# A planner that counts TensorE's changes between fp32 and half precision, with due times chosen anew

## The chip, the cores and the metric

The kernel runs on one core of a Trainium2 chip. TensorE (PE) multiplies matrices, VectorE (DVE) and ScalarE (ACT) work on elements, GpSimd (POOL) does almost nothing here, and SyncE (SP) issues the transfers (DMA). The metric is the device time of one execution, in microseconds; lower is better. Several runs are made, and their median counts. One more execution is recorded by the hardware profiler, and the views below are of it.

## What is computed

A layer-normalised input `xn` (2048 positions, 512 channels) goes two ways, and the results are multiplied:

```
xn = layernorm(u)
# A: a state-space convolution along the 2048 positions
K[d, l] = real(sum_n C[d,n] * exp(dt[d]*A[d,n]*l) * dt[d]*B[d,n])
s = irfft(rfft(xn, 2L) * rfft(K, 2L))[:L] + xn * Dskip
# B: token mixing by shifts, then an MLP of width 1376
h  = gelu(layernorm(xn) @ w1)
x1 = xn + shifted(h) @ w2          # the four quarters of h shifted by +1, -1, +2, -2
b  = x1 + gelu(layernorm(x1) @ w3) @ w4
out = u + s * silu(b)
```

All inputs and the output are fp32.

## The kernel before

**The stages.** `params` makes the parameters of the states. `token_mixing` does the first layer norm, the product with `w1` (tiles `xT`, `w`, `hT`), the first stage of the input's transform (`u_stage1`, tiles `X`, `ks`, output `ue`), the product with `w2` (`hs_pair`), the scales and half-precision copies of `w3` and `w4` (`prep`, tiles `w3h` and `w4h`), and the second layer norm (`ln_second`). `tables` builds the exponentials and the sines of 16 groups of 32 channels (tiles `mag`, `pt`, `kt`, `eg`; mostly VectorE and ScalarE) and sums over the states on TensorE (`sums`: 64 small fp32 matmuls in each of 32 units, into banks `pc`), which gives `K`; it goes to memory by `kev`. `kstage1` does the first stage of `K`'s transform (`ksl`, output `k1e`). `products` does the second stage of both transforms (units named `kin` and `uin`), multiplies them (`kh`, `pr`) and starts the way back (unit `pr`, output `z1e`). `inverse` ends it (`zin`) and multiplies into `X`; `finish` adds the input and stores.

The channels come in two halves, `hf` 0 and 1: `tables(0)`, `kstage1(0)`, `products(0)`, then the same for 1. The MLP has 8 groups of 256 positions, and each has six steps `jp`: 24 matmuls with `w3h`, a gelu on ScalarE (`g`), a split into two halves-precision parts (`ghl`, ScalarE and VectorE), and 12 matmuls with `w4h` into banks `pa`. Before a group, `mlp_input` normalises and transposes it (`x1n`, `x1T`).

**The two kinds of matmul.** The products with `w3` and `w4` take half-precision operands (f16, three matmuls for each product). Everything else on TensorE is fp32, the transposes too. The units have several shapes on the array: 128*128 (MLP, transposes, `w1`, `w2`), 128*64 (`kin`, `uin`), 64*128 (`pr`), 128*32 (`kt`, `pt`), 32*64 (`ks`), 64*32 (`zin`); the first number is rows, the second columns.

**The planner.** The program above does not issue instructions. It calls `Plan.add`, which notes each unit with the engines that may do it, its cost on each, and what it depends on. Units made under `plan.together` are one piece. `due(t)` sets the due time of the units that follow: `t` from constants such as `M0 + MC*g` for the MLP, `T0 + TC*cc` for the tables, `PA`, `PB` for the products, plus an entry of `SHIFT`, one for each call of `due` (353 numbers).

`Plan.order` then plays the program through with the costs. Whichever engine can start something first takes, of the units that are ready, the one with the lowest score: its due time, plus `SWITCH` where ScalarE would have to load another table of functions, plus `PREFER`, `AVOID` and their like where a unit may go to ScalarE or VectorE. The order in which each engine took its units is the order in which `issue` writes them, so it is the order on each engine's queue. A transfer is taken to land `LAND` after it ran; a table load costs ScalarE `TABLE_LOAD` in the play. Nothing of it exists on the chip but the order and the choice of engine. All instructions come from one line of `issue`, line 310, so views by line name L310 for all, and the tiles tell them apart.

Of the kernel before, what the change touches and what calls it, by code (L numbers as in the profile page):

```python
# [11 lines left out]
F16 = mybir.dt.float16  # L12
# [71 lines left out]
class Op:  # L84
# [9 lines left out]
LATENCY = {"PE": 0.23, "ACT": 0.16, "DVE": 0.13, "SP": 0.0}  # L94
SAME = {"PE": 0.0, "ACT": 0.13, "DVE": 0.1, "SP": 0.0}
TABLE_LOAD = 1.41
DMA_RATE = 300e3
LAND, PAD = 2.45, 0.16
BASE, FINE, END = 16512, 19840, 229368

KGC, QUAD = 3.25, 0.95
WARM = 40

SHIFT = (
    -2357, -12777, -7728, -8471, -1890, -5820, 626, 2299, 7826, 2606, 3103, -2484, -1642, 1374, 635, 1552,
    -5430, 4370, -2565, 2626, -1860, 4424, 2714, -4679, -3803, -2285, -3146, -4248, -5241, 213, 2051, 3978,
    9221, 3207, 1433, -2296, -2539, -178, 2374, 2140, 9495, 265, 2415, -4317, 2024, -5695, -4424, -1536, 1044,
    -3874, -412, 1369, -3390, -64, 1033, 83, -9702, 2535, -4187, 5182, -2767, -1991, -4017, 4504, -1834, 1373,
    -7030, -1888, 1509, -961, -638, -116, -8830, -3284, -147, 833, 3202, -866, 6815, 1881, -776, -1517, 8158,
    -2771, 3388, 7167, 2300, 9228, -1206, 5040, 884, 683, 384, 6727, -5917, 5434, 3924, 949, -40, 143, 1079,  # L110
    -6875, 971, 1037, -3725, -7917, 838, -5291, -3043, -2915, -1908, 3046, -1796, 231, -7429, -6152, -1811,
    -1498, -1748, -918, 3362, -1195, 68, -5613, -1298, -4707, -5318, 3932, -9853, 445, 2154, -4838, 45, -1328,
    1607, 5499, 892, -1606, 5826, -1702, 7543, -2199, -4457, 17060, 1309, 1934, 2210, 2592, -2979, -373, -4584,
    -3271, -1323, 5435, -4525, 7358, 6315, -28, 1908, 1745, 4555, -2473, -3546, 3446, -71, 3791, 3269, 3699,
    -4728, 1638, -208, 25, -3832, -1734, -7872, -6249, 1060, 1013, 154, 1376, 711, 1802, -4989, 787, 4474,
    -3057, -6935, 5895, -975, -3716, -68, 425, -1428, -1701, -608, 7719, -860, -1822, 1535, -3182, -2129, -2825,
    8377, 4060, -1121, -638, -3207, -9351, -1721, 6415, 3544, -2559, -84, -2122, 2999, 522, -1386, 8061, 10306,
    11912, 1524, -3127, -5785, -1486, -5228, -3327, 535, -2675, 2538, 770, -868, -964, -8884, 1422, -375, -549,
    413, 674, 777, 1357, 1723, -707, 1664, 2958, 2189, 2194, -4655, 4203, 1477, -692, 7608, 1024, 2389, -6548,
    3086, 1289, 4001, -5674, -2103, -2325, 191, 2535, 7638, 5247, 3899, -3574, -7476, 10, -12299, 2768, -6779,  # L120
    -7700, 8670, -577, -2655, -5094, -2963, -6991, -1665, 4621, -1517, 976, 2193, 955, 1168, -2284, -7221, 1774,
    2110, 2001, 886, 2377, -6284, -3310, -1104, -4085, -5416, -8519, -1464, 4322, -4518, -2765, 5960, -916,
    -5164, -4685, 2304, -8462, 5438, -879, 2434, -4976, -7337, -8426, 5719, -1100, -913, -157, 3264, -3332,
    -7127, 3616, 9378, -2152, 10830, -7314, -2047, -1665, 2199, -4364, 5296, 1040, -1366, -2191, 4626, -3019,
    -2281, -367, 1901, 236, 1460, -997, 2115, 2661, -1551, -3533, -5930, 1634, 1890, 6703, 8932, 2028, -4182,
)
Q0, QC = -778.0, 0.05
SWITCH = 2279.26
PREFERP, AVOIDP = 2674.41, 272.51
PREFER, AVOID = 3332.92, 790.65  # L130
PV, T0, TC = 257.0, 396.7, 309.52
LX, LC, LP, LW, LV = -4000.0, 0.11, -3964.6, -2693.7, -3696.7
M0, MC, WC = 807.9, 710.86, 0.25
H0, HC, SC = -3530.1, 638.4, 0.22
KA, PA, PAC, FA = -1045.1, -3015.7, 0.25, 592.1
KB, PB, PBC, FB = -157.1, -136.4, 0.08, 323.0
FC = 0.29


def mlp_due(g, jp):  # L140
# [3 lines left out]
class Plan:  # L144
# [50 lines left out]

    def add(self, alts, writes, reads, table=0, nbytes=0):
        op = self.group or self.new(table, nbytes)
        op.psum = "PSUM" in str(reads[0].space) if reads else False
        for e, (cost, call) in alts.items():
            old = op.alts.setdefault(e, [0.0, []])  # L200
            old[0] += cost
            old[1].append(call)


        def after(other, name):
            if other[0] is not op:
                op.deps.add(other[0].idx)
                if other[1] != name:
                    op.alias.add(other[0].idx)

        for ap in reads:
            me = (op, ap.tensor.name)
            for c in self.cover(ap):
                if isinstance(c, str):
                    op.deps.update(self.cells[c])
                    continue
                st = self.cells.setdefault(c, [None, {}])
                if st[0] is not None:
                    after(st[0], me[1])
                if c[1] == "bank":  # L220
                    for r in st[1].values():
                        after(r, me[1])
                    st[0], st[1] = me, {}
                else:
                    st[1][op.idx] = me
        for ap in writes:
            me = (op, ap.tensor.name)
            for c in self.cover(ap):
                if isinstance(c, str):
                    self.cells.setdefault(c, []).append(op.idx)  # L230
                    continue
                st = self.cells.setdefault(c, [None, {}])
                if st[0] is not None:
                    after(st[0], me[1])
                for r in st[1].values():
                    after(r, me[1])
                st[0], st[1] = me, {}
# [12 lines left out]
    def order(self):  # L250
        ops = self.ops
        for op in ops:
            op.succ, op.n, op.ready, op.eng = [], len(op.deps), 0.0, None
        for op in ops:
            for d in op.deps:
                ops[d].succ.append(op)
        pools = {e: [] for e in self.engines}
        free = dict.fromkeys(self.engines, 0.0)

        def release(op):  # L260
            for e in op.alts:
                pools[e].append(op)

        for op in ops:
            if op.n == 0:
                release(op)
        table, dma, out = 0, 0.0, []
        while len(out) < len(ops):
            t, e = min(
                (max(free[e], min(o.ready for o in pool)), e) for e, pool in pools.items() if pool  # L270
            )
            pick, score = None, None
            for o in pools[e]:
                if o.ready <= t + 0.02:
                    v = o.vt
                    if e == "ACT" and o.table and o.table != table:
                        v += SWITCH
                    if len(o.alts) > 1:
                        on = (PREFERP, AVOIDP) if o.psum else (PREFER, AVOID)
                        v += on[e != "DVE"]  # L280
                    if pick is None or (v, o.idx) < score:
                        pick, score = o, (v, o.idx)
            for k in pick.alts:
                pools[k].remove(pick)
            pick.eng = e
            pick.cost, pick.calls = pick.alts[e]
            cost = pick.cost
            if e == "ACT" and pick.table and pick.table != table:
                table = pick.table
                cost += TABLE_LOAD  # L290
            pick.start = t
            free[e] = t + cost
            if e == "SP":
                dma = max(dma, free[e] + 0.9) + pick.nbytes / DMA_RATE
                done = dma + LAND
            else:
                done = free[e]
            out.append(pick)
            for s in pick.succ:
                s.n -= 1  # L300
                s.ready = max(s.ready, done + (SAME[e] if list(s.alts) == [e] else LATENCY[e] + PAD))
                if s.n == 0:
                    release(s)
        self.span = max(max(free.values()), dma)
        return out
# [21 lines left out]
def pe_cost(name, args):  # L327
    f = 1 if args[2].dtype == F16 else 4
    return 0.11 if name == "transpose" else columns(args[2]) * f / 2400.0 + 0.0025 * (1 + f // 4)
# [25 lines left out]
class Engine:  # L355
# [3 lines left out]
    def __getattr__(self, name):  # L359
        def call(*args, **kw):  # L360
# [6 lines left out]
            table, nbytes = 0, 0  # L367
            if self.eng == "PE":
                cost = pe_cost(name, args)
            elif self.eng == "ACT":  # L370
                cost = act_cost(args, kw)
                if name == "activation":
# [47 lines left out]
def kernel(  # L420
# [405 lines left out]
    def products(hf):  # L826
# [3 lines left out]
        for un in range(NG // (2 * nb)):  # L830
# [28 lines left out]
            for b in range(nb):  # L859
# [12 lines left out]
                V.tensor_add(z[1], z[1], t[1][:, 1])  # L872
                due()
                pz = [t[:, :DH] for t in bank[3]]
                with plan.together(cost=0.9):
                    for ri in range(2):
                        for a in range(2):
                            h = slice(64 * a, 64 * a + 64)
# [370 lines left out]
```

## Time and profile before

| | us |
|---|---|
| median of 3 runs | 673.19 |
| lowest and highest run | 671.51, 675.04 |
| the profiled execution | 671.43 |
| its span, first to last instruction | 669.7 |

The mean granted TensorE clock is 0.965 of full speed. Matmuls are pipelined, so a row of the timeline overlaps the next: the time that a unit takes of TensorE is read from the start of one row to the start of the next. Rows of a timeline have the start, the time, the engine, the line, the operation, output<-inputs, the array's rows*columns, the moving operand with its type, and the count; idle time before a row stands in brackets with what ended it.

### The profile page before, as it was taken

The page shows a single profiled execution, that of the slowest core. Times are in us where ns is not written, and L with a number is a line of the kernel's source. Part 1 is how long each engine was busy: PE and PEld are TensorE (multiplying, and loading weights), DVE is VectorE, ACT ScalarE, POOL GpSimd, SP SyncE. Part 2 cuts the span into 40 slices and gives each one's busy share as a digit, 9 for nine tenths or more (in the row PEclk, how much of TensorE's full clock was granted, in tenths as well). Part 3 has the DMA queues.
Part 4 walks back from the last instruction along what each step waited for, and adds up shares of the span by engine and source line. Part 5 has one row for each costly group of instructions (what it writes and reads, how often), then busy time and mean ns, then how long its engine had stood idle before and what let it go on. Part 6 is the DMA issues. An engine that isn't in the chain of part 4 may idle for free.

```text
span 669.7 us, 13855 instructions
## 1 busy us (share of the span) xinstructions
PE 629.2 (94%) x5526; PEld 416.4 (62%) x5526; DVE 540.2 (81%) x798; ACT 479.8 (72%) x1050; POOL 0.7 (0%) x6
## 2 busy tenths in 40 slices
PE   7699989999995998998999999999999999999984
PEld 7567758466464785665687576676675756556531
DVE  5898999999999999988999999997434155454557
ACT  3989899969849999987999999994245363223420
POOL 0000000000000000000000000000000000000000
PEclk9899979999997999998999999999999999999995
DMA  8945342421022120385343314328599468844997
GB/s 258 244 132 188 107 162 93 144 98 55 32 80 79 32 61 21 80 221 173 78 137 100 97 60 125 103 75 211 168 249 276 135 148 215 205 155 142 236 315 219
DMA packets 98063, 95.60 MB, mean 143 GB/s; under 512 B 48272, under 2 KB 77968, under 8 KB 97104
## 3 DMA queue, kind: packets, MB, share of 16 engines
q1 hardware_dynamic: 98000, 94.73, 50.2%
q8 instruction: 43, 0.70, 0.4%
q14 instruction: 20, 0.16, 0.1%
HBM read 61.16 MB, written 33.55 MB: 141 GB/s over the span
## 4 chain that ended last, share of the span: by engine, by line
PE 54%; DVE 32%; DMA 6%; ACT 4%; issue 3%; SPq 1%; DVEq 0%; ACTq 0%
PE pb L310 19%; PE pa L310 12%; PE pc L310 12%; PE pd L310 11%; DVE pt L310 10%; DVE X L310 4%; DVE kt L310 4%; DMA X<-in_A_u_dram 2%; DVE pr L310 2%; DVE ghl L310 2%; DVE stats L310 2%; DVE eg L310 2%; DMA zin<-scr_Zda 1%; SPq L310 1%; DVE pab L310 1%
## 5 line engine op out<-in xcount | busy, mean ns | idle before, releaser
L310 PE MATMUL pb<-x1T,w3h 128*128 128x256 f16 (+1 forms) x1056 | 126.0, 275 | 1.1 <-DVE w3h L310 1.1
L310 PE MATMUL pa<-w4h,ghl 128*128 128x512 f16 (+1 forms) x528 | 124.5, 383 | 1.1 <-DVE w4h L310 0.8
L310 PEld LDWEIGHTS <-w3h 128*128 128x128 f16 (+1 forms) x1056 | 102.8, 101 | 30.2 <-issue 15.4
L310 ACT ACT_TABLE_LOAD x85 | 109.1, 1283 | 2.5 <-PEq L1237 0.7
L310 PEld LDWEIGHTS <-ghl 128*128 128x128 f16 (+1 forms) x528 | 49.2, 98 | 67.5 <-issue 16.2
L310 ACT ACTIVATE mag<-par 128x64 f32<-128x64 f32 x512 | 84.0, 272 | 6.3 <-DVE pt L310 6.1
L310 PE MATMUL pc<-kt 128*32 128x64 f32 x1024 | 84.6, 415 | 0.6 <-DVE kt L310 0.6
L310 PE MATMUL pc<-pt 128*32 128x64 f32 x1024 | 78.4, 387 | 0.0
L310 PE MATMUL pb<-xT,w 128*128 128x256 f32 x256 | 61.1, 396 | 1.4 <-ACT hT L310 1.4
L310 DVE SCALAR_TENSOR_TENSOR ghl<-g,wsc,ghl 128x512 f16<-128x512 f32 (+1 forms) x48 | 35.3, 750 | 31.0 <-ACT ghl L310 30.7
L310 PEld LDWEIGHTS pb<-xT,w 128*128 128x128 f32 x256 | 50.0, 199 | 15.8 <-issue 6.8
L310 PEld LDWEIGHTS pc<-pt 128*32 128x32 f32 x1024 | 56.8, 194 | 0.1
L310 PEld LDWEIGHTS pc<-kt 128*32 128x32 f32 x1024 | 48.8, 175 | 9.6 <-issue 6.2
L310 ACT ACTIVATE g<-pb,wsc 128x512 f32<-128x512 f32 (+1 forms) x48 | 32.8, 692 | 26.8 <-PE pb L310 26.5
L310 ACT ACTIVATE ghl<-g,wsc 128x512 f16<-128x512 f32 (+1 forms) x32 | 22.6, 714 | 27.0 <-PE pa L310 26.9
L310 DVE TENSOR_TENSOR kt<-mag,kt 128x1024 f32<-128x1024 f32 x32 | 41.6, 1300 | 0.0
L310 DVE SCALAR_TENSOR_TENSOR pt<-kt,pt 128x2080 f32<-128x2080 f32 x16 | 37.7, 2359 | 0.1
L310 ACT COPY z1e<-pd 128x256 f32<-128x256 f32 x36 | 12.7, 389 | 34.0 <-PE pd L310 34.0
L310 DVE TENSOR_TENSOR pr<-pc,kh 128x512 f32<-128x512 f32 x32 | 21.0, 686 | 19.4 <-PE pc L310 16.7
L310 PE MATMUL pd<-pr,cst 64*128 64x256 f32 x256 | 36.3, 402 | 0.0
L310 ACT ACTIVATE kt<-kt,halfpi 128x2080 f32<-128x2080 f32 x16 | 33.0, 2063 | 0.0
L310 DVE COPY z1e<-pd 128x256 f32<-128x256 f32 x28 | 11.6, 441 | 25.9 <-PE pd L310 25.9
(159 smaller groups left out, 990.7 us busy)
## 6 DMA issues: line engine op xcount, KB each, us to landing
wst<-in_B_w_dram SPq DMA_DIRECT2D x20, 512.0 KB, 3.7
scr_Ud<-ue SPq DMA_DIRECT2D x16, 512.0 KB, 3.1
scr_Kfa<-k1e SPq DMA_DIRECT2D x16, 256.0 KB, 3.6
uin<-scr_Ud SPq DMA_DIRECT2D x32, 128.0 KB, 3.1
cst<-c_gp SPq DMA_DIRECT2D x16, 256.0 KB, 2.8
kin<-scr_Kfa SPq DMA_DIRECT2D x32, 128.0 KB, 2.7
scr_Zda<-z1e SPq DMA_DIRECT2D x16, 256.0 KB, 2.3
xr<-in_A_u_dram SPq DMA_DIRECT2D x16, 256.0 KB, 6.3
```

Of the source, the lines that this page charges most:

```text
L310: ins = [getattr(self.engines[op.eng], name)(*args, **kw).ins for name, args, kw in op.calls]
```

## The change

Three parts. First, the planner keeps a kind for TensorE as it keeps a table for ScalarE: 1 for units with half-precision operands, 2 for fp32. In the play, a unit of the other kind costs `TURN` = 0.1 us more, and its score is raised by `KIND`. A unit made under `together` takes the kind of its members. Second, two costs of the play: `LAND` from 2.45 to 2.75, and the `pr` unit of `products` from 0.9 to 1.0. Third, all constants of the due times and all 353 numbers of `SHIFT` have other values, and so have the weights `SWITCH`, `PREFER` and `AVOID`.

```diff
+TURN = 0.1
-LAND, PAD = 2.45, 0.16
+LAND, PAD = 2.75, 0.16
 SHIFT = (
-    -2357, -12777, -7728, -8471, -1890, -5820, 626, 2299, 7826, 2606, 3103, -2484, -1642, 1374, 635, 1552,
+    -15363, -41919, 3148, -7770, -4886, -7327, 5312, 10411, 10508, 20269, 11828, -21285, -10539, -11177, -1968,
...
-SWITCH = 2279.26
-PREFERP, AVOIDP = 2674.41, 272.51
-PREFER, AVOID = 3332.92, 790.65
-PV, T0, TC = 257.0, 396.7, 309.52
-M0, MC, WC = 807.9, 710.86, 0.25
-H0, HC, SC = -3530.1, 638.4, 0.22
-KA, PA, PAC, FA = -1045.1, -3015.7, 0.25, 592.1
-KB, PB, PBC, FB = -157.1, -136.4, 0.08, 323.0
+SWITCH = 12026.4
+KIND = 1975.3
+PREFERP, AVOIDP = 8567.89, -14706.0
+PREFER, AVOID = 10606.8, 10381.4
+PV, T0, TC = 2239.0, 2383.7, 1852.46
+M0, MC, WC = 12644.9, 2568.54, 0.07
+H0, HC, SC = -4082.3, 1063.72, 0.11
+KA, PA, PAC, FA = -6598.1, -29218.2, 0.14, 13134.1
+KB, PB, PBC, FB = 9962.3, -12822.4, 0.32, 7956.4
...
     def add(self, alts, writes, reads, table=0, nbytes=0):
         op = self.group or self.new(table, nbytes)
+        op.table = op.table or table
...
-        table, dma, out = 0, 0.0, []
+        table, dma, out = {"ACT": 0, "PE": 2}, 0.0, []
+        change = {"ACT": (SWITCH, TABLE_LOAD), "PE": (KIND, TURN)}
...
-                    if e == "ACT" and o.table and o.table != table:
-                        v += SWITCH
+                    if e in table and o.table and o.table != table[e]:
+                        v += change[e][0]
...
-            if e == "ACT" and pick.table and pick.table != table:
-                table = pick.table
-                cost += TABLE_LOAD
+            if e in table and pick.table and pick.table != table[e]:
+                table[e] = pick.table
+                cost += change[e][1]
...
             if self.eng == "PE":
                 cost = pe_cost(name, args)
+                table = 1 if args[2].dtype == F16 else 2
...
-                with plan.together(cost=0.9):
+                with plan.together(cost=1.0):
```

## What I expect, before seeing the result

> **What bounds the kernel now.** I read the page's busy totals, clock line and chain first, then the busy time by stage, and then TensorE's timeline, since the change names TensorE.
>
> ```profile
> span 669.7 us, 13855 instructions
> PE 629.2 (94%) x5526; PEld 416.4 (62%) x5526; DVE 540.2 (81%) x798; ACT 479.8 (72%) x1050; POOL 0.7 (0%) x6
> PEclk9899979999997999998999999999999999999995
> PE 54%; DVE 32%; DMA 6%; ACT 4%; issue 3%; SPq 1%; DVEq 0%; ACTq 0%
> ```
>
> TensorE is busy 94% of the span and carries 54% of the chain that ended last, VectorE 32%. The clock line dips in several slices. The stretches say where each engine sets the pace.
>
> ```profile
> 90.00:211.00 121.00, 115.34 (x1018) 75.10 (x1006) 120.70 (x163) 102.69 (x298) 0.00 (x0) 0.98 0.27 88
> 211.00:226.00 15.00, 11.71 (x78) 9.70 (x79) 15.00 (x16) 12.88 (x15) 0.00 (x0) 0.68 0.15 49
> 226.00:400.00 174.00, 168.59 (x1749) 116.01 (x1748) 169.02 (x195) 162.24 (x347) 0.00 (x0) 0.99 0.36 101
> 400.00:640.00 240.00, 239.43 (x2064) 150.18 (x2063) 140.70 (x231) 124.50 (x230) 0.00 (x0) 1.00 0.66 177
> 640.00:670.00 30.00, 17.71 (x194) 5.83 (x192) 19.34 (x32) 3.57 (x4) 0.00 (x0) 0.73 0.86 254
> ```
>
> The columns are PE, PEld, DVE, ACT, POOL busy us, granted clock, DMA share and GB/s. From 90 to 226 VectorE is full (135.7 of 136 us). From 226 to 400 TensorE, VectorE and ScalarE are all within 7% of full. From 400 to 640 TensorE is full at full clock (239.43 of 240), and the other two have 100 us to spare. There only less TensorE time can shorten the kernel. The last 30 us are a tail of TensorE remnants, VectorE additions and output transfers.
>
> **What the change removes and adds.** No operation is added to or taken from the list: the 5526 matmuls, their shapes and transfers stay. What moves is the order in which each queue takes units, whether ScalarE or VectorE does a unit that both can do, and with it how many of ScalarE's table loads there are. So the sum has two terms: fewer changes on TensorE, and holes filled or opened by a new order.
>
> **Term 1, the changes on TensorE.** What one costs:
>
> ```profile
> 501.42 1.46 PE L310 MATMUL pa<-w4h,ghl 128*128 128x512 f16 x6
> 502.72 1.47 PE L310 MATMUL pb<-x1T,w3h 128*128 128x256 f16 x12
> ...
> 550.30 1.47 PE L310 MATMUL pa<-w4h,ghl 128*128 128x512 f16 x6
> 551.70 1.08 PE L310 MATMUL pc<-uin,cst 128*64 128x256 f32 x8
> 552.72 1.14 PE L310 MATMUL pd<-pr,cst 64*128 64x256 f32 x8
> 553.78 1.08 PE L310 MATMUL pc<-kin,cst 128*64 128x256 f32 x8
> 554.80 1.47 PE L310 MATMUL pa<-w4h,ghl 128*128 128x512 f16 x6
> ```
>
> A start-to-start distance is what a unit takes of TensorE. Six half-precision matmuls take 1.30 us before more halves (501.42 to 502.72) and 1.40 before fp32 (550.30 to 551.70): entering fp32 costs 0.10. A lone spectrum unit takes 1.02 (551.70 to 552.72), and a pr unit between two others 1.06.
>
> ```profile
> 406.74 1.08 PE L310 MATMUL pd<-kin,cst 128*64 128x256 f32 x8
> 407.65 1.03 PE L310 MATMUL pd<-uin,cst 128*64 128x256 f32 x8
> 408.62 2.79 PE L310 MATMUL pb<-x1T,w3h 128*128 128x256 f16 x24
> ...
> 514.00 5.34 PE L310 MATMUL pa<-w4h,ghl 128*128 128x512 f16 x24
> 519.18 0.60 PE L310 MATMUL pb<-ident,x1n 128*128 128x128 f32 x4
> 519.62 1.47 PE L310 MATMUL pb<-x1T,w3h 128*96 128x256 f16 x12
> ```
>
> Two spectrum units in a row take 1.88 (406.74 to 408.62), so two that are joined save 2 x 1.02 - 1.88 = 0.16 and one entry of 0.10: 0.26 together. But the transposes of x1n are fp32 and cost nothing on either side: 24 pa before them take 5.18, or 0.216 each, as in 1.30 / 6, and four transposes take 0.44. They have the 128*128 shape of most of the halves (the last MLP tile has 96 columns or rows). And pr followed by kin, both fp32, costs 1.06, no less than a unit that halves follow. So what is paid for is the change of the array's shape, not of the number format. Joining two fp32 units of different shapes saves the one entry, 0.10, and no more.
>
> The Trainium skill says this too: "TensorEngine Tiling (Array Packing)", Key Properties, has a change of tiling mode, not of the tile alone, drain TensorE. By that rule the planner's count of formats misses fp32 units that follow each other in different shapes, and charges the transposes for nothing; the rows above agree on both.
>
> How many there are: I read TensorE's timeline from the first unit of halves to the last.
>
> ```profile
> 217.16 10.99 PE L310 MATMUL pb<-x1T,w3h 128*128 128x256 f16 x84
> ...
> 625.29 0.66 PE L310 MATMUL pd<-zin,is 64*32 64x256 f32 x16
> 625.75 0.64 PE L310 MATMUL pc<-zin,is 64*32 64x256 f32 x16
> 626.32 1.48 PE L310 MATMUL pb<-x1T,w3h 128*128 128x256 f16 x12
> 627.73 0.66 PE L310 MATMUL pd<-zin,is 64*32 64x256 f32 x16
> 628.33 1.47 PE L310 MATMUL pa<-w4h,ghl 96*128 96x512 f16 x6
> ...
> 646.65 2.77 PE L310 MATMUL pa<-w4h,ghl 128*128 128x512 f16 x12
> 649.34 0.66 PE L310 MATMUL pd<-zin,is 64*32 64x256 f32 x16
> ```
>
> Between these ends there are 74 runs of halves, so 148 changes; 135 of them change the shape as well. Of the fp32 runs, 9 are a stage-1 unit of the kernel's transform (ksl) alone, 8 an inverse unit (zin) alone, 8 a pr alone, 3 a kin and 3 a uin alone. Two zin joined take 1.03 (625.29 to 626.32), a single one 0.60 (627.73 to 628.33): joining saves 0.17 and an entry, 0.27. If the 9 ksl become 4 runs, the 8 zin 3, the six lone spectra 3, and the 8 pr join spectra of another shape: 5 x 0.27 + 5 x 0.27 + 3 x 0.26 + 8 x 0.10 = 4.3 us. That is the upper end; below, it is nothing, or a loss as in the slower rival. The pr units cannot all be joined: in the first half pr, kin and uin of the next block share TensorE's banks d and wait for the copies out of them, and halves fill that wait. I take 2.5 us, about 60%, since some of the ksl runs lie before 400, where VectorE and ScalarE are nearly as full and TensorE's gain is not the end's. The weight on a change, KIND = 1975, is only a ninth of the spread of the new SHIFT (18,265 standard deviation, from the diff), so it decides among units that are nearly equal. That speaks for a small number of joins, unless the due times do the joining.
>
> **Term 2, the order.** The largest hole of TensorE behind the first 90 us:
>
> ```profile
> 206.09 0.61 PE L310 MATMUL pc<-pt 128*32 128x64 f32 x8
> 212.90 1.97 PE L310 MATMUL pd<-ident,x1n 128*128 128x128 f32 x8 [6.20 <-ACT x1n L310]
> 216.26 1.11 PE L310 MATMUL pd<-ident,x1n 128*128 128x128 f32 x4 [1.39 <-ACT x1n L310]
> ```
>
> TensorE has run out of table sums, and the MLP cannot begin until VectorE has finished the second layer norm behind table work. It idles 6.20 + 1.39 = 7.6 us, and the clock falls: 0.68 granted over the 15 us of the row above, 4.8 us of full-speed work lost. Together 12.4 us. Filling it needs the layer norm's VectorE work earlier, or table work that feeds TensorE kept for it; the new constants move both (M0 to T0, H0, HC). A hole filled there is worth its full price only if VectorE, full up to 226, isn't later for it. Bounds: 12.4 gained to the same lost, if it doubles. I take a third, 4 us: VectorE's 169 of 174 us in the next stretch takes most of a gain back. The tail I leave as it is: its additions hang on each other whatever the order. The first 90 us I leave too, as inputs land there.
>
> Table loads move with the order as well:
>
> ```profile
> L310 ACT ACT_TABLE_LOAD x85 | 109.1, 1283 | 2.5 <-PEq L1237 0.7 <-PE pb L310 0.4
> ```
>
> At 1.28 us each, the 11.8 us that ScalarE has to spare between 226 and 400 cover some 9 more; ten fewer there would free 13 us of ScalarE, with VectorE still full beside it. I put nothing on them; their effect either way is inside the bounds of the holes.
>
> The planner's other prices (2.75 instead of 2.45 us for a transfer to land, 1.0 instead of 0.9 for pr) move nearer to rows: pr takes 1.06. They cost no instruction; their effect is in term 2.
>
> **Sum.** 671.43 (the profiled execution; its span is 669.7, so 1.7 lie around it) - 2.5 - 4 = 664.9. The median of the three runs is 673.19, 1.8 above the profiled one, so I expect 666.7 for a median.
>
> **The rivals.**
> First, that it doesn't do what it says: kinds run longer, but shapes change as often, fp32 to fp32, at the same 0.10, and the holes only move. For it: the transposes, and the shape changes between fp32 units that the planner still counts as free. Against it: joins of equal shape do save 0.26. Then 0 to 1 us: 672.5.
>
> Second, the hole is closed entirely: 12.4 from it and 4.3 from joins are 16.7; 673.19 - 16.7 = 656.5. For it: the MLP's start depends on layer-norm work of few instructions, which a due time can bring forward. Against it: VectorE is full on both sides. "TensorE: Matmul & The Clock Gate" of the Trainium skill, Part 1, gives about 3.4 us of idling before the clock halves. The trace agrees that 6.2 was enough; a gap cut below that would keep the clock, which is in the 12.4 already.
>
> Third, slower: the halves are spent too early. They are the filler while the second half's spectra are being written and read back:
>
> ```profile
> 523.37 2.79 PE L310 MATMUL pb<-x1T,w3h 128*128 128x256 f16 x24
> 526.09 1.08 PE L310 MATMUL pc<-uin,cst 128*64 128x256 f32 x8
> 527.11 8.04 PE L310 MATMUL pb<-x1T,w3h 128*128 128x256 f16 x72
> 534.98 6.64 PE L310 MATMUL pa<-w4h,ghl 128*128 128x512 f16 x30
> 541.54 1.08 PE L310 MATMUL pc<-kin,cst 128*64 128x256 f32 x8
> ```
>
> For 14.4 us (527.11 to 541.54) TensorE runs nothing but halves, with one uin unit done and the first kin unit still to come. It decides when less than 14.4 us of halves is ready at that point, for example because runs were lengthened before it. If half of them are missing, TensorE idles 7.2 us, and the clock takes a loss like the 4.8 above: +12; less 2.5 for joins, 682.7. Against it: from 523.4 to the end the timeline holds 288 pb and 168 pa, at 7.87 / 72 = 0.109 and 0.217 us, 68 us in all, nearly five times what is needed. But halves are ready only as fast as ScalarE and VectorE evacuate the ones before, and a new order may have left fewer.
>
> **How the numbers follow.** About half a per cent, 3.4 us, is what a measurement of this kernel can tell from no change. The forecast (666.7, and its neighbours to 669.8) gets 0.42, the hole closed 0.20, no fewer shape changes 0.20, the filler spent early 0.18. So faster 0.62, same 0.20, slower 0.18. The range takes in the forecast and both rivals up to the edge of the third: below, 656.5 less the 1.7 between the lowest run (671.51) and the median; above, 673.19 and 3.8, a third of the 12 us that the third rival would cost. That is 654.8 to 677.0, and leaves 0.18 out.
>
> **What would show it.** The changes of format between the first half and the last in TensorE's timeline: about 148 less 30 to 50 if term 1 is right, with ksl and zin units in rows of two or more; the shape changes among fp32 units beside them. Unit prices must stay (0.109, 0.217, 1.02, 1.06). Term 2: the wait of pd for x1n, now 7.6 us, at some 5, and the clock there above 0.68. The third rival would show as a wait of TensorE for kin or uin behind the last ksl. I am wrong if TensorE's idle time grows elsewhere by what the hole loses, or if the tail behind the last half, now 20 us (649.3 to 669.7), is not the same.

## The result and the profile after

The changed kernel takes 669.71 us (median of 19 runs, 666.94 to 671.56) beside 672.16 us of the kernel before on the same chips (19 runs, 670.92 to 675.04). The ratio is 0.9947, with a 95% interval of 0.9935 to 0.9960: faster by half a per cent, some 3.6 us. The forecast was 666.7 in a range of 654.8 to 677.0, so the direction was right and the gain about half of what I expected. Its profiled execution took 666.94 us, the lowest of the 19, so the two profiles lie 4.5 us apart where the medians lie 2.5 apart and the ratio says 3.6.

The head of the page of the changed kernel, with its span, busy totals, clock in 40 slices and chain by engine:

```profile
span 665.2 us, 13827 instructions
PE 627.9 (94%) x5526; PEld 416.4 (63%) x5526; DVE 537.5 (81%) x794; ACT 467.3 (70%) x1043; POOL 0.7 (0%) x6
PEclk9889979999998999999999999999999999999995
PE 44%; DVE 43%; DMA 4%; issue 4%; ACT 4%; SPq 1%; DVEq 0%
```

TensorE has the same 5526 matmuls and 1.3 us less busy time. The totals of VectorE and ScalarE fell by 2.7 and 12.5 us; 11 table loads fewer (74, at 1.28 us each) are 14 us less, more than the whole fall of ScalarE. The share of the chain moved from TensorE to VectorE.

The busy time by stretch, in the columns of before:

```profile
211.00:226.00 15.00, 12.81 (x94) 10.86 (x95) 14.96 (x16) 14.58 (x17) 0.00 (x0) 0.78 0.14 45
226.00:400.00 174.00, 167.53 (x1759) 116.56 (x1758) 172.42 (x201) 154.18 (x349) 0.00 (x0) 1.00 0.39 105
400.00:640.00 240.00, 239.67 (x2080) 149.71 (x2077) 135.28 (x224) 122.17 (x223) 0.00 (x0) 1.00 0.67 187
640.00:670.00 30.00, 13.93 (x154) 4.75 (x152) 16.42 (x27) 1.57 (x2) 0.00 (x0) 0.73 0.53 148
```

The picture is that of before: TensorE full from 400 to 640, VectorE nearly full ahead of that. The hole is still there, a little shorter, with the clock at 0.78 instead of 0.68. (The clock is of one execution only: in the second profiles used below, the same stretch has 0.72 in the changed kernel and 0.71 in the one before.) Its rows in TensorE's timeline, with the idle time in brackets:

```profile
211.47 1.97 PE L318 MATMUL pd<-ident,x1n 128*128 128x128 f32 x8 [5.45 <-DVE x1n L318]
214.85 1.09 PE L318 MATMUL pd<-ident,x1n 128*128 128x128 f32 x4 [1.41 <-ACT x1n L318]
```

6.86 us of idling instead of 7.6; 6.24 in the second profile, where the kernel before has 7.6 again.

And the number that the change is about: read from TensorE's timeline, 140 changes of format instead of 148, and 129 of them with a change of shape instead of 135. The shape changes between two fp32 units rose from 82 to 85. So the changes of shape fell from 217 to 214 over the whole kernel. (The expectations below count them in the plan, unit by unit, and have 211 for these 214.)

**Where the difference lies.** Three marks of the timelines cut each profile in three: the start of the first matmul of the MLP, the start of the last one (w4h), and the end of the span. A second profile of each kernel (the runs before_again and again below) shows how far the pieces hold.

| us | before | before_again | changed | again |
|---|---|---|---|---|
| start to the first MLP matmul | 217.2 | 217.0 | 215.7 | 216.4 |
| from there to the last MLP matmul | 431.9 | 431.8 | 430.5 | 431.2 |
| from there to the end of the span | 20.6 | 20.6 | 18.9 | 18.7 |
| span | 669.7 | 669.4 | 665.2 | 666.3 |

Between the means of the pairs: 1.05 us ahead of the MLP, 0.97 in the long middle, 1.80 in the tail. The tail's part can be read from VectorE's additions of the input (X<-X,xr), eight of them, one for each pair of output rows, and each followed by its output transfer. First the changed kernel's timeline, then that of the kernel before, each from the first addition near the last MLP matmul to the last one:

```profile
637.86 1.22 DVE L318 TENSOR_TENSOR X<-X,xr 128x1024 f32<-128x1024 f32 x1
645.66 1.23 DVE L318 TENSOR_TENSOR X<-X,xr 128x1024 f32<-128x1024 f32 x1
...
657.32 1.23 DVE L318 TENSOR_TENSOR X<-X,xr 128x1024 f32<-128x1024 f32 x1
659.30 1.23 DVE L318 TENSOR_TENSOR X<-X,xr 128x1024 f32<-128x1024 f32 x1
```

```profile
647.59 1.23 DVE L310 TENSOR_TENSOR X<-X,xr 128x1024 f32<-128x1024 f32 x1
651.43 1.21 DVE L310 TENSOR_TENSOR X<-X,xr 128x1024 f32<-128x1024 f32 x1
...
661.81 1.23 DVE L310 TENSOR_TENSOR X<-X,xr 128x1024 f32<-128x1024 f32 x1
663.80 1.23 DVE L310 TENSOR_TENSOR X<-X,xr 128x1024 f32<-128x1024 f32 x1
```

At the end a pair leaves every 1.98 us (657.32 to 659.30). The changed order has one pair out at 637.86, ahead of the last MLP matmuls; the kernel before has none out until 647.59. One pair fewer in the row of 1.98 us steps is the size of what the tail gained, 1.8. TensorE's timeline has the same: six zin units behind the last half in the changed kernel (646.55 to 657.01), seven in the kernel before (649.34 to 661.50).

### The profile page after: what moved, and what is told of

It reads as the page before. It is cut to its first block, busy times and chain, and to the rows that moved or that the text cites. A ratio compares the mean times of both kernels' runs of the same rounds, so it can differ in the third digit from the quotient of the medians.

```text
span 665.2 us, 13827 instructions
## 1 busy us (share of the span) xinstructions
PE 627.9 (94%) x5526; PEld 416.4 (63%) x5526; DVE 537.5 (81%) x794; ACT 467.3 (70%) x1043; POOL 0.7 (0%) x6
## 4 chain that ended last, share of the span: by engine, by line
PE 44%; DVE 43%; DMA 4%; issue 4%; ACT 4%; SPq 1%; DVEq 0%
DVE pt L318 14%; PE pb L318 13%; PE pa L318 11%; PE pc L318 11%; PE pd L318 8%; DVE kt L318 7%; DVE X L318 4%; DVE pr L318 3%; DMA X<-in_A_u_dram 2%; DVE eg L318 2%; DVE pab L318 2%; DVE stats L318 2%; DVE ghl L318 2%; ACT L318 1%; SPq L318 1%
## 5 line engine op out<-in xcount | busy, mean ns | idle before, releaser
L318 PE MATMUL pa<-w4h,ghl 128*128 128x512 f16 (+1 forms) x528 | 121.9, 380 | 0.0
L318 PE MATMUL pb<-xT,w 128*128 128x256 f32 x256 | 63.1, 404 | 3.5 <-DMA w<-in_B_w_dram 1.9
L318 PEld LDWEIGHTS pc<-kt 128*32 128x32 f32 x1024 | 48.2, 176 | 12.4 <-issue 8.8
L318 ACT ACTIVATE ghl<-g,wsc 128x512 f16<-128x512 f32 (+1 forms) x40 | 27.4, 689 | 27.7 <-PE pa L318 27.5
L318 ACT COPY z1e<-pd 128x256 f32<-128x256 f32 x42 | 14.5, 385 | 37.3 <-PE pd L318 32.1
L318 DVE SCALAR_TENSOR_TENSOR pt<-kt,pt 128x2080 f32<-128x2080 f32 x16 | 40.4, 2523 | 0.1
L318 DVE TENSOR_TENSOR pr<-pd,kh 128x512 f32<-128x512 f32 x32 | 23.6, 749 | 13.8 <-ACT kh L318 12.1
```

Source lines behind the costliest of these rows:

```text
L318: ins = [getattr(self.engines[op.eng], name)(*args, **kw).ins for name, args, kw in op.calls]
```

## The experiments

### What a change of format costs, and what a change of shape

Matmuls without a use are put behind the last output:

```diff
...
+    with plan.together():
...
+        for a, b in ((H, F128), (H, F64), (H, H64), (F128, F64)):
+            for n in (1, 8):
+                for k in range(8 // n):
+                    for f in (a, b):
+                        for i in range(n):
+                            f()
```

> The changed kernel, with matmuls behind the last output: 12 halves of 128x256 on the full array (H), 4 fp32 on the full array (F128), 8 fp32 on 128x64 tiles (F64), 12 halves on 128x64 tiles (H64). Four pairs, each eight times in turn and then eight of the one and eight of the other: 14 changes fewer. If a change of shape is what costs, taking turns is longer by about 14 x 0.1 = 1.4 us for H and F64, H and H64, F128 and F64, and by nothing for H and F128. If a change of number format is what costs (the planner's view), it is longer by 1.4 us for H and F128 and for H and F64, and by nothing for H and H64 and for F128 and F64.

Three of the pairs in TensorE's timeline, first in turn, then eight and eight. H and F128 differ in format alone:

```profile
694.43 1.89 PE L318 MATMUL pc<-X,ident 128*128 128x256 f32 x8
696.15 1.47 PE L318 MATMUL pa<-w3h 128*128 128x256 f16 x12
697.47 1.89 PE L318 MATMUL pc<-X,ident 128*128 128x256 f32 x8
699.20 10.64 PE L318 MATMUL pa<-w3h 128*128 128x256 f16 x96
709.67 13.98 PE L318 MATMUL pc<-X,ident 128*128 128x256 f32 x64
...
723.49 1.47 PE L318 MATMUL pa<-w3h 128*128 128x256 f16 x12
```

H and H64 differ in shape alone, and F128 and F64 too:

```profile
787.53 1.49 PE L318 MATMUL pa<-w3h 128*128 128x256 f16 x12
788.94 0.85 PE L318 MATMUL pb<-w3h 128*64 128x256 f16 x12
789.72 1.48 PE L318 MATMUL pa<-w3h 128*128 128x256 f16 x12
791.14 0.84 PE L318 MATMUL pb<-w3h 128*64 128x256 f16 x12
791.91 10.65 PE L318 MATMUL pa<-w3h 128*128 128x256 f16 x96
802.50 5.43 PE L318 MATMUL pb<-w3h 128*64 128x256 f16 x96
807.86 1.99 PE L318 MATMUL pc<-X,ident 128*128 128x256 f32 x8
809.78 1.95 PE L318 MATMUL pd<-X,ident 128*64 128x256 f32 x16
811.66 1.99 PE L318 MATMUL pc<-X,ident 128*128 128x256 f32 x8
...
838.27 14.08 PE L318 MATMUL pc<-X,ident 128*128 128x256 f32 x64
852.28 14.03 PE L318 MATMUL pd<-X,ident 128*64 128x256 f32 x128
```

Format alone: a pair in turn takes 3.04 us (694.43 to 697.47), and 10.47 / 8 + 13.82 / 8 = 3.04 in blocks. It costs nothing. Shape alone, in halves: 2.19 in turn (787.53 to 789.72), 10.59 / 8 + 5.36 / 8 = 1.99 in blocks; 0.20 for a pair, 0.10 for a change. Shape alone, in fp32: 3.80 in turn (807.86 to 811.66), 14.01 / 8 + 14.03 / 8 = 3.50 in blocks (no row follows the last block, so its 14.03 is the row's own time; the same block of the pair H and F64 takes 13.97 from start to start, which gives 3.50 too); 0.15 for a change. Both together (H and F64, 3.29 in turn against 3.07) are no dearer than shape. So the planner's TURN has the right size, on the wrong thing. The rule of the Trainium skill that the prediction named ("TensorEngine Tiling (Array Packing)", Key Properties) is that a change of tiling mode drains TensorE. The trace agrees in all three pairs, as time is lost where the shape changes and nowhere else.

### Joining units of one shape

A pass behind the planner takes a TensorE unit earlier, where the plan has it ready and that joins two of one shape. Only TensorE's queue changes.

```diff
+            if shape(b) != a:
+                for j in range(i + 1, min(i + 1 + reach, len(pe))):
+                    c = pe[j]
+                    if shape(c) != a or c.ready > b.start + slack:
+                        continue
+                    if any(pos[d] >= pos[b.idx] for d in c.deps):
+                        continue
+                    if changes(pe[:i] + [c] + pe[i:j] + pe[j + 1 :]) < changes(pe):
+                        out.remove(c)
+                        out.insert(out.index(b), c)
+                        break
...
-        for op in self.order():
+        for op in self.joined(self.order(), 4, 0.5):
```

> The changed kernel, and behind the planner a pass that takes a TensorE unit up to four places earlier where that joins two units of one shape and the plan has it ready; the orders of the other queues stay. In TensorE's order 211 changes of shape become 166 and 140 changes of format 102. If changes cost TensorE time that the end waits for, 45 x 0.1 = 4.5 us less at most than the changed kernel, 2 to 4.5 with some of them before 400 us: a ratio to the kernel before of 0.988 to 0.992. Rival: a unit that is taken earlier keeps one waiting that ScalarE or VectorE needs, and the gain is given back: 0.994 or more.

Measured: 1.0132 of the kernel before (1.0093 to 1.0170), 13 us slower than the changed kernel. The rival's bound (0.994 or more) holds, but far more than the gain was given back. The busy time of its stretch from 400 to 640, its longest waits of TensorE behind 400 (the second and third lie mostly in the tail, and the changed kernel has such waits there too), and one place in the timeline:

```profile
400.00:640.00 240.00, 229.50 (x1980) 148.05 (x1979) 131.79 (x214) 117.92 (x233) 0.00 (x0) 1.00 0.61 168
```

```profile
PE pd L349 <- ACT z1e L349: 3.7, 6, 0.8
PE pd L349 <- DVE X L349: 3.1, 3, 1.6
PE pc L349 <- DVE X L349: 2.7, 2, 2.1
```

```profile
563.85 1.13 PE L349 MATMUL pd<-pr,cst 64*128 64x256 f32 x8
565.73 1.13 PE L349 MATMUL pd<-pr,cst 64*128 64x256 f32 x8 [0.75 <-ACT z1e L349]
566.79 1.08 PE L349 MATMUL pc<-kin,cst 128*64 128x256 f32 x8
567.71 1.03 PE L349 MATMUL pc<-uin,cst 128*64 128x256 f32 x8
568.57 1.08 PE L349 MATMUL pc<-kin,cst 128*64 128x256 f32 x8
570.20 1.08 PE L349 MATMUL pc<-uin,cst 128*64 128x256 f32 x8 [0.56 <-DVE pr L349]
```

TensorE is busy for 229.50 instead of 239.67 us. Two pr units in a row wait 0.75 us for ScalarE to copy the first out of the bank; a fourth spectrum unit in a row waits 0.56 for VectorE to read the one whose bank it takes. A join that saves 0.10 to 0.26 costs 0.5 to 0.8 where the unit taken out from between had covered such a copy. Between the first MLP matmul and the last, TensorE idles 20.2 us instead of 7.0; 11.5 us of that are 19 waits for VectorE or ScalarE to empty a bank (z1e, X, pr, kh, k1e), and the changed kernel has none of these there.

With moves past one unit only, and no slack:

> As the run with joined units, but a unit is moved past one other unit only, and only if the plan has it ready at that unit's start: 194 changes of shape instead of 211, 128 of format instead of 140. If what cost 13 us there is cover that was lost, and moves of this kind lose none: 17 x 0.1 = 1.7 us less than the changed kernel, 0.992. If they lose cover as well: 0.996 to 1.005.

Measured: 0.9978 (0.9956 to 1.0001), 0.3% above the changed kernel. These moves lose cover as well; the expected gain of 1.7 us isn't there. Six waits for the emptying of a bank, 3.7 us together, stand against the 17 x 0.1 = 1.7 us; the difference of 2.0 is the size of what the run is longer by.

### Far more weight on a change

```diff
-KIND = 1975.3
+KIND = 40000.0
```

> The changed kernel with KIND at 40000, twenty times as much: 86 changes of format and 166 of shape in the plan. If fewer changes are worth 0.1 us each: 45 x 0.1 = 4.5 us below the changed kernel, 0.987. If the halves between fp32 units are cover, as the run with joined units says: above 1.03, with TensorE idle behind 400 us.

720.60 us in one run, 1.07 of before. The stretch behind 640, and the longest waits of TensorE in the whole span:

```profile
640.00:720.00 80.00, 46.55 (x484) 21.51 (x480) 42.02 (x83) 10.91 (x26) 0.00 (x0) 0.77 0.89 256
```

```profile
PE pd L318 <- DMA zin<-scr_Zda: 7.0, 1, 7.0
PE pb L318 <- DVE x1T L318: 6.5, 4, 3.6
```

The MLP is done 84.8 us before the end, not 18.9: the halves came early, in long runs, and what is left is a chain of fp32 units with nothing to cover its copies and transfers. TensorE is busy for 46.55 us of the 78.8 behind 640. The wait of 7.0 us lies there, with others of 4.9 and 2.9 us for zin's transfers; those for x1T lie ahead of the last MLP matmul. This is my slower rival in kind, the filler spent early, though the transfers waited for are zin's, and not kin's or uin's as I had said. Of the weights tried in the changed kernel it shows at this one alone, twenty times the change's.

### Each part of the change without the others

The counting off, in the changed kernel:

```diff
-TURN = 0.1
+TURN = 0.0
...
-KIND = 1975.3
+KIND = 0.0
```

> The changed kernel with KIND and TURN at 0: its due times and its other costs, no counting of changes. The plan then has 142 changes of format and 212 of shape (140 and 211 with the counting). If the new due times and not the counting carry the gain, about the changed kernel's time: 0.993 to 0.997 of the kernel before. If the counting carries it, 1.000. As the due times were chosen for a plan with the counting, the other order may also be worse by chance, above 1.000.

Measured: 1.0022 (1.0003 to 1.0041). The orders in the trace are those of the changed kernel up to some 248 us, and so is the time: 215.5 us to the first MLP matmul, as there, but 436.5 from it to the last one (430.5).

The counting alone, in the kernel before (the lines of the change, with KIND at 374):

> The kernel before with the counting alone: TURN 0.1 and KIND 374, which has the same ratio to SWITCH as in the change; due times and costs as before. The plan has 160 changes of format and 222 of shape (148 and 216 before), as one other choice early moves all that follow. If the counting as such is a gain: 0.995 or less. If a due time is good only with the order it was chosen in: 1.005 to 1.03.

Measured: 1.0111 (1.0073 to 1.0150).

The two costs of the play as before, in the changed kernel:

```diff
-LAND, PAD = 2.75, 0.16
+LAND, PAD = 2.45, 0.16
...
-                with plan.together(cost=1.0):
+                with plan.together(cost=0.9):
```

> The changed kernel with the two costs of the play as before: LAND 2.45, pr 0.9. The counting and the new due times stay. The plan has 138 changes of format and 210 of shape. If the gain is of the due times and the counting: 0.993 to 0.998. If the due times are good only in the one plan that they were chosen for, as the two other partial kernels suggest: 1.005 to 1.03.

Measured: 1.0408 (1.0354 to 1.0462), worse than expected: 231.7 us to the first MLP matmul and 451.7 from it to the last.

The counting alone doesn't give the gain, and without the counting, or without the two costs, it is gone; the new due times without both weren't run. The reason that I see, argued and not shown: 353 due times fit one run of the play; another weight or cost makes one unit go first that went second, and all that follow are drawn in another order, for which the numbers were not chosen. These runs say that the parts belong together. They don't say what a part would be worth with due times of its own.

### The hole ahead of the MLP

Matmuls of the identity, which nothing reads, fill the hole in the changed kernel; the other orders stay.

```diff
         ln_second(slice(0, S))
+        vt, plan.vt = plan.vt, 1e8
+        with plan.together(cost=0.0):
+            T.matmul(bank[0][1][:, :S], ident, mv[:, :, 0], start=True, stop=True)
+            for k in range(18):
+                T.matmul(bank[0][1][:, :P], ident, ident, start=True, stop=True)
+        plan.vt = vt
```

> The changed kernel with 18 more matmuls of the identity (3.9 us at full clock) in TensorE's hole ahead of the first x1n transposes, started by the last mean and variance; nothing reads them. If the half clock behind the hole (6.8 us in the changed kernel's profile, 6.1 of them over work) is part of what sets the end, the clock stays full there and the time falls by up to 3 us: ratio to before about 0.990. If VectorE sets the pace until 400 us, nothing changes: 0.9947. If the extra matmuls hold up the transposes, it is slower than the changed kernel.

Measured: 0.9946 (0.9925 to 0.9967), the changed kernel's own. First its timeline behind the hole, then the changed kernel's:

```profile
207.84 4.26 PE L318 MATMUL pa<-ident 128*128 128x128 f32 x36
...
216.01 5.40 PE L318 MATMUL pb<-x1T,w3h 128*128 128x256 f16 x48
222.55 3.65 PE L318 MATMUL pb<-x1T,w3h 128*128 128x256 f16 x32 [1.13 <-ACT g L318]
```

```profile
215.73 6.33 PE L318 MATMUL pb<-x1T,w3h 128*128 128x256 f16 x48
222.37 5.40 PE L318 MATMUL pb<-x1T,w3h 128*128 128x256 f16 x48 [0.30 <-ACT g L318]
```

The clock stayed up at the hole: the first 48 matmuls take 5.40 instead of 6.33 us. Then TensorE waits 1.13 instead of 0.30 us for the first gelu, and both go on at the same place, 222.4 and 222.6. A wait took the place of the one removed. "TensorE: Matmul & The Clock Gate" of the Trainium skill, Part 1, asks for no idle gaps above some 3.4 us. At the hole the trace agrees: with gaps of 0.70 and 2.27 us left, the clock stayed, and that brought no time. But the limit isn't a safe one: in the same profile a stretch of 3.4 us at half clock (from 251.6) follows a gap of 1.93 us, and in the two profiles of the kernel before one (from 309.3 and 308.4) follows gaps of 1.82 and 2.01 us. The measurement decides.

The other way, 66 instead of 18:

> As the run with 18 matmuls in the hole, but with 66 (14.4 us at full clock): the first transposes and the MLP behind them start about 10 us later, with the clock full. If TensorE's time there is the end's, about 10 us less 3 for the clock: 7 us slower than the changed kernel, 1.005. If VectorE sets the pace there, at most 2 us slower: 0.995 to 0.998.

Measured: 1.0086 (1.0055 to 1.0118). The first MLP matmul is at 225.3, 9.6 later than in the changed kernel's profile, and the span is 675.2, 10.0 longer. So a delay of the MLP's start reaches the end in full, and VectorE being full there hides none of it: its own queue holds MLP units in a fixed order, and waits with them (9.1 us in one piece for x1T, where it waits for nothing between 205 and 240 us in the changed kernel). Time added to the hole has its full price. That time taken out of it would be gained in full isn't shown. The hole's clock had no price in the changed kernel, because of the gelu behind it.

### The two kernels once more

> The changed kernel once more, unchanged. Time as on record, 0.9947 of the kernel before (0.9935 to 0.996). Its profile shows how much of the difference between the two profiles (4.5 us) is of one execution: if the stretches at half clock fall otherwise in each execution, the new profile has another number of them than 7 windows of 3.4 us ahead of the tail, and another time with it; if they belong to the order, the same ones.

Measured: 0.9935 (0.9902 to 0.9967). Ahead of the tail the record of the granted clock in the trace has 27.3 us at half speed; the first profile of the same kernel had 23.9. The stretches come in steps of 3.4 us and fall differently in each execution (10.2 us at the hole here and 6.8 in the first; 10.2 in both profiles of the kernel before).

> The kernel before once more, for a second profile. If the three pieces of the difference belong to the orders, this profile has them where the first had: the first MLP matmul at 217 +- 1 us, 431.8 +- 0.7 us from it to the last w4h matmul, 20.7 +- 0.5 us from that to the end.

671.21 us; the three pieces are in the table above, as expected. So the order sets them, to within 0.7 us, and the span of one kernel differs by 0.3 and 1.1 us between its two profiles.

## Why the prediction was right in sign and half in size

**What bounds it.** Right: the stretches stayed as they were, and TensorE from 400 to 640 is full in both.

**Luck in the sign.** The time fell within the range and the right way, but not for the reasons of the sum. Of the 3.8 us between the pairs of profiles, 1.8 came in the tail, on which the sum put nothing; the other 2.0 alone would be under the 3.4 us that I had called the least that can be told from no change. Both signs that I had named for being wrong also show. TensorE's idle time in the middle grew by what the hole lost: 7.0 and 7.1 us instead of 5.9 and 6.2, where the hole lost 1.05. And the tail behind the last half isn't the same (the table's 18.9 and 18.7 us for 20.6).

**The price of a change.** Right: 0.10 us, for the shape and not for the format, is what the matmuls in turn show; between fp32 units it is 0.15.

**Term 1, 2.5 us.** This is the step that failed first, and by its count. I expected 30 to 50 changes fewer; there are 8 fewer, and 3 fewer of shape. At 0.10 that is 0.3 us over the kernel, or 0.7 for the 7 fewer (177 for 184) between the first MLP matmul and the last. I had seen that KIND is small beside the spread of SHIFT, and still took 60% of an upper end. The upper end of 4.3 us was wrong as well, as it took a join for a gain wherever it could be made. 45 fewer changes by the joining pass cost 13 us: in 19 places TensorE then waits for a bank to be emptied, and the changed order has none of these waits. The count was off as well: six inverse units lie alone between halves (627.73 to 646.05 us), not 8, which takes 0.5 us from the 4.3. I had said so of the pr units of the first half alone.

**Term 2, 4 us from the hole.** Right in kind, and mis-sized: 1.05 us instead of 4. TensorE's last table sum ends at 206.7 and 206.5 us in the kernel before, 206.0 and 207.3 in the changed one, the same place on average; the first transposes begin at 212.9 and 212.8, and at 211.5 and 212.1. So the 1.05 us ahead of the MLP are the hole's idle time, on average. The 4.8 us for the clock were wrong twice. The stretch at half clock (210.3 to 220.5) was counted in part over idle time that was priced already: 3.3 us of it behind 211, so 3.1 us of work were lost, not 4.8. And the clock was worth nothing in the changed kernel, as the filled hole shows: ScalarE's gelu ends the next wait. So of the 12.4 us that I priced, at most the 7.6 of idle time were to be had. A gap under 3.4 us, which I had taken to keep the clock, does not always do so, as the 1.82 us above shows. The argument that a full VectorE takes most of a gain back found no support: a start later by 9.6 us cost 10.0.

**The tail, "left as it is".** Wrong. It gave 1.8 us, the largest of the three pieces, and one output pair that left before the MLP ended is the size of it. The first 90 us, left out too, are where the hole's 1.05 us come from, by VectorE's busy time. From 90 to 211 VectorE, whose layer norm ends the hole, is busy for 120.7 or 120.8 of 121 us in all four profiles; in the first 90 it is busy for 77.7 and 76.6 us in the changed kernel and 75.5 and 75.7 in the one before, so it idles some 1.6 us less there, and its work ahead of the first transposes is 198 to 199 us in all four. Which unit moved I haven't isolated.

**The rivals.** The first, that kinds are hardly longer and shapes change as often, describes TensorE's order better than the forecast did; its time, 672.5, was wrong, since the gain came from elsewhere. The closed hole did not come. The filler spent early is real at KIND = 40000, and absent here: a run of 84 + 24 halves (522.0 to 536.5 us) still lay where the second half's spectra had to land.

**What stays open.** The middle's 0.97 us is near the size of its fewer changes (0.7), but idle time and clock differ there by as much: 1.0 us more of idle time, and against it no stretch at half clock near 309, which in both profiles of the kernel before follows an idle time of 1.8 or 2.0 us (in the first, 12 matmuls with w4h take 4.38 us there, 308.50 to 312.88, instead of 2.59). So that cause is argued and not shown. Whether due times chosen as long without the counting would do as well wasn't tried, so it isn't shown that the counting was needed. And whether a search whose play counts changes of shape would find more wasn't tried.

## What to carry to other kernels

Price a switch by what the hardware switches, and check it on two units that differ in that alone: here number formats mix for nothing, and array shapes cost 0.10 to 0.15 us. Before you collect units of one kind, ask what the unit between them covers, since a bank's copy of 0.5 to 0.8 us outweighs several switches. Where hundreds of due times were chosen for one plan, a part of the plan can't be judged by undoing it alone, and a gain should be looked for in pieces of the timeline, the tail among them, and not where the change is aimed.

## What the runs showed of the hardware, not expected

- fp32 and half-precision matmuls of one shape follow each other with no loss: 3.04 us for a pair in turn and in blocks.
- A change of shape between fp32 units costs 0.15 us, more than between halves (0.10).
- Executions of one kernel differ in where the clock is halved: 23.9 and 27.3 us ahead of the tail in two profiles, with spans of 665.2 and 666.3 us.
- A stretch of 3.4 us at half clock can follow a short gap: TensorE had idled 1.82 and 2.01 us ahead of it in the two profiles of the kernel before, and 1.93 in the one with the filled hole. A gap of 2.22 us in the first profile of the changed kernel (247.7) was followed by none.
